# A Fourier filter and a gated feed-forward on one core: wider folding and filter operations, normalised rows kept in DRAM, eleven pairs of block products, and one written order

## The chip, the core and the metric

The kernel runs on one core of a Trainium2 chip. The time is device microseconds from the first to the last instruction of one execution; three runs of the kernel before gave 399.61, 400.31 and 401.77, and their median, 400.31, is what the change is measured against. One execution was also taken by the hardware profiler; its rows name the engines PE (matrix products), PEld (weight loads of PE), DVE (vector), ACT (scalar and activation), POOL (the third element-wise engine) and SP (which issues most DMA transfers).

## What is computed

```python
def _A_ref(x, w_r, w_i):                       # x: 1 x 2048 x 512
    X = rfft2(x) * (w_r + 1j * w_i)            # w: 2048 x 257
    return irfft2(X, (2048, 512))
def _B_ref(x, W_gate, W_up, W_down):           # F = 1376
    gate, up = x @ W_gate, x @ W_up
    return ((gate * (gate > 0)) * up) @ W_down

x = A_x
xn = _layernorm(x)
s = _A_ref(xn, A_w_r, A_w_i)
g = _silu(_B_ref(xn, B_W_gate, B_W_up, B_W_down))
return x + s * g
```

## The kernel before, in words

**Rows and blocks.** x is 2048 rows by 512 columns, held as 16 tiles of 128 rows. Two tiles together are a unit c = 0 … 7 of 512 KB: it is loaded, its mean and deviation are taken (`deviations`, L534), and `normalise` (L556) writes the normalised rows xf. Four tiles are a block of the feed-forward, c = 0 … 3.

**Numbers.** Every product has float16 operands. A float32 value is split into a high part (rounded to float16) and a low part (the rest), mostly a copy on ACT and a subtraction on DVE, and each product is done in three passes (`PASSES`: high·high, high·low, low·high).

**Feed-forward.** `turn` (L571) and `turn_row` (L632) make the transposed rows xT of a block. `product` (L953) multiplies them with gate and up weights (wgu), for 11 tiles f of 128 hidden columns (the last, TAIL, has 96): PE rows gu, groups of twelve matmuls 128x512. `hidden` (L1011) forms relu(gate)·up and splits it into h; `down` (L1032) multiplies h with the down weights wds into dn. The f tiles are taken in `PAIRS` (0,1), (3,4), (5,6), (7,8), (2,9). For some pairs and blocks `fast_products` (L1060) does not form the four products of twelve 512-wide matmuls but seven of twelve 256-wide ones (sa, sb, sc), by a scheme of Strassen's kind with sums and differences of row blocks (xS, made by `row_sums`, L595: sums on DVE, splits, two DMA writes to S_d and two transposing reads) and of weight blocks (wT and rp, made by `weight_sums`, L799). `FASTS` says for how many of the last blocks this is done, pair by pair.

**Filter branch.** The transform of the 512 columns and 2048 rows is done as products with small cosine and sine matrices. `fold` (L662) forms even and odd parts of xf (eo, ee, xs), `split` makes them float16, `first_stage` (L699) is the group s1 on PE (64-row products), whose results go to A_d in DRAM. Eight chunks q (`fft_chunk`, L1142) then load at from A_d and do y, xx, the filter (xsp, tt, pf), z and v, and store to C_d; the filter of a chunk is wt, scaled by cw (`filter_scale`, L895). `last_stage` (L1304) loads ct from C_d, does s2 on PE and unfolds it (zz, ae, ye, sv) to the rows s; `finish` (L1353) multiplies with the gate g and adds x. All eight first stages come before the first chunk, and all chunks before the first last stage; the feed-forward's products fill PE in between, so most filter steps lie on DVE, ACT and POOL while PE works on gu and dn.

**Order.** The functions do not issue instructions; they append steps (`step`, L236) with an engine, a cost, what they read and write, and a due time. `Plan.run` (L255) then places the steps: a list scheduler with modelled costs, a table DUES with a due time for each step, a table WAITS with the lead of loads, and rules for ports, buffers and changes of PE between 64-row and 128-row products. The result is the order in which instructions are issued to each engine, and each engine works through its own list in that order. Because all instructions go through one helper, most profile rows name its line, L200 before and L155 after.

Two short places say what the fast pairs are:

```python
def fast(c, n):
    return c >= NBL - int(FASTS[n])     # NBL = 4 blocks
FASTS = ['2', '1', '2', '2', '2']       # before: nine pairs
```

Of the kernel before, what the change touches and what calls it, by code (L numbers as in the profile page):

```python
# [1572 lines left out]
```

## Time and profile before

| what | value |
|---|---|
| runs | 399.61, 400.31, 401.77 us (median 400.31) |
| span of the profiled execution | 399.6 us |
| mean granted clock of PE | 0.996 |
| PE busy | 391.2 us (98%) |
| DVE busy | 329.2 us (82%), 726 instructions |
| ACT busy | 247.2 us (62%), 479 instructions |
| POOL busy | 72.3 us (18%), 79 instructions |
| DMA | 69.55 MB, 174 GB/s in the mean |

How to read the rows below. A row of the groups names line, engine, operation, output <- inputs, shape and count, and after the bar the busy time in us, the mean of one instruction in ns, and the idle time ahead of such instructions with what ended it. A row of a timeline has the start, the length in us, the engine, and how many instructions it joins. A row of the windows has the stretch in us, its length, the busy time of PE, PEld, DVE, ACT and POOL with instruction counts, the granted clock of PE, the DMA share and GB/s. Matmuls overlap, so the mean of one is longer than the distance between two.

### The profile page before, as it was taken

The page shows a single profiled execution, that of the slowest core. Times are in us where ns is not written, and L with a number is a line of the kernel's source. Part 1 is how long each engine was busy: PE and PEld are TensorE (multiplying, and loading weights), DVE is VectorE, ACT ScalarE, POOL GpSimd, SP SyncE. Part 2 cuts the span into 40 slices and gives each one's busy share as a digit, 9 for nine tenths or more (in the row PEclk, how much of TensorE's full clock was granted, in tenths as well). Part 3 has the DMA queues.
Part 4 walks back from the last instruction along what each step waited for, and adds up shares of the span by engine and source line. Part 5 has one row for each costly group of instructions (what it writes and reads, how often), then busy time and mean ns, then how long its engine had stood idle before and what let it go on. Part 6 is the DMA issues. An engine that isn't in the chain of part 4 may idle for free.

```text
span 399.6 us, 8608 instructions
## 1 busy us (share of the span) xinstructions
PE 391.2 (98%) x3332; PEld 243.8 (61%) x3332; DVE 329.2 (82%) x726; ACT 247.2 (62%) x479; POOL 72.3 (18%) x79
## 2 busy tenths in 40 slices
PE   6999999999999999999999999999999999999995
PEld 5965444544445444456585777776567878787544
DVE  3899998998888997669986888988769863887995
ACT  6997986868576666845568865535335542754422
POOL 1004300000000000051405391413212301122211
PEclk9899999999999999999999999999999999999999
DMA  7972311327812998997878790536543048998496
GB/s 272 407 230 63 106 54 34 100 55 178 294 55 51 307 307 244 279 268 167 215 222 246 223 241 22 146 81 199 153 125 107 2 106 183 228 296 167 133 239 158
DMA packets 59353, 69.55 MB, mean 174 GB/s; under 512 B 24688, under 2 KB 36560, under 8 KB 59312
## 3 DMA queue, kind: packets, MB, share of 16 engines
q1 hardware_dynamic: 57872, 66.38, 57.2%
q0 software_dynamic: 1440, 2.62, 4.3%
q8 instruction: 26, 0.43, 0.4%
q14 instruction: 15, 0.12, 0.1%
HBM read 43.81 MB, written 22.56 MB: 166 GB/s over the span
## 4 chain that ended last, share of the span: by engine, by line
PE 82%; DVE 8%; DMA 4%; ACT 3%; issue 2%; SPq 0%; DVEq 0%; ACTq 0%; POOLq 0%
PE dn L200 26%; PE gu L200 26%; PE sb L200 8%; PE sc L200 5%; PE sa L200 5%; PE z L200 3%; PE xx L200 3%; PE s L200 2%; DVE wgu L200 2%; PE y L200 2%; PE v L200 2%; DMA out<-sv 2%; DMA x<-in_x 2%; DVE sv L200 1%; ACT wgu L200 1%
## 5 line engine op out<-in xcount | busy, mean ns | idle before, releaser
L200 PEld LDWEIGHTS <-wgu 128*128 128x128 f16 x960 | 93.0, 98 | 65.3 <-issue 2.9
L200 PE MATMUL dn<-wds,h 128*128 128x512 f16 (+2 forms) x528 | 118.2, 373 | 0.3 <-DVE h L200 0.3
L200 PE MATMUL gu<-xT,wgu 128*128 128x512 f16 (+1 forms) x528 | 112.0, 369 | 0.4 <-DVE xT L200 0.4
L200 PEld LDWEIGHTS <-h 128*128 128x128 f16 (+1 forms) x594 | 53.5, 98 | 54.4 <-issue 2.8
L200 POOL TENSOR_TENSOR rp<-rp,rp 128x512 f32<-128x512 f32 x9 | 12.1, 1354 | 132.9 <-DVE pw L200 125.5
L200 PEld LDWEIGHTS <-wT 128*128 128x128 f16 x324 | 31.2, 98 | 6.1 <-issue 1.0
L200 PE MATMUL sb<-xS,wT 128*128 128x256 f16 x216 | 26.6, 273 | 0.0
L200 PE MATMUL sa<-xT,wgu 128*128 128x256 f16 x216 | 26.5, 273 | 0.0
L200 ACT ACTIVATE r<-gu 128x512 f32<-128x512 f32 (+2 forms) x26 | 14.9, 574 | 16.2 <-PE gu L200 16.2
L200 DVE TENSOR_TENSOR h<-gu,r 128x512 f32<-128x512 f32 (+3 forms) x34 | 20.6, 607 | 5.0 <-ACT h L200 3.5
L200 ACT ACTIVATE h<-h 128x512 f16<-128x512 f32 (+1 forms) x26 | 16.1, 624 | 11.8 <-DVE h L200 11.8
L200 DVE SCALAR_TENSOR_TENSOR tt<-xsp,cw,wt 128x512 f32<-128x512 f32 x32 | 22.8, 755 | 0.1
L200 ACT ACTIVATE g<-dn,cdi 128x512 f32<-128x512 f32 (+1 forms) x16 | 10.8, 673 | 16.5 <-PE dn L200 16.5
L200 DVE TENSOR_TENSOR h<-h,h 128x512 f16<-128x512 f32 (+1 forms) x26 | 18.3, 705 | 1.8 <-ACT h L200 1.7
L200 POOL TENSOR_TENSOR tt<-tt,tt 128x256 f32<-128x256 f32 x10 | 9.5, 957 | 43.1 <-DVE tt L200 41.1
L200 PE MATMUL gu<-xT,wgt 128*64 128x256 f16 (+1 forms) x144 | 17.0, 309 | 0.0
L200 ACT ACTIVATE a<-y 128x1024 f16<-128x1024 f32 x8 | 8.2, 1024 | 12.8 <-PE y L200 6.1
L200 DVE SCALAR_TENSOR_TENSOR wgu<-raw,p,wgu 128x512 f16<-128x512 f32 x20 | 15.1, 772 | 0.0
L200 POOL TENSOR_TENSOR pf<-tt,tt 128x256 f32<-128x256 f32 x12 | 11.3, 947 | 18.9 <-DVE tt L200 16.6
L200 DVE TENSOR_TENSOR a<-y,a 128x1024 f16<-128x1024 f32 x8 | 9.8, 1224 | 5.6 <-ACT a L200 5.5
L200 ACT ACTIVATE rp<-rp,csc 128x512 f32<-128x512 f32 x20 | 13.5, 713 | 1.1 <-DMA rp<-in_wg 1.1
L200 PEld LDWEIGHTS <-wgt 128*64 128x64 f16 (+1 forms) x144 | 9.6, 106 | 6.6 <-issue 1.3
(208 smaller groups left out, 701.2 us busy)
## 6 DMA issues: line engine op xcount, KB each, us to landing
A_d<-t SPq DMA_DIRECT2D x16, 256.0 KB, 3.8
rw<-in_wl SPq DMA_DIRECT2D x8, 512.0 KB, 5.2
wt<-in_wl SPq DMA_DIRECT2D x8, 512.0 KB, 5.5
at<-A_d SPq DMA_DIRECT2D x8, 512.0 KB, 5.1
C_d<-t SPq DMA_DIRECT2D x16, 256.0 KB, 3.5
ct<-C_d SPq DMA_DIRECT2D x16, 256.0 KB, 6.8
x<-in_x SPq DMA_DIRECT2D x7, 512.0 KB, 5.7
G_d<-g SPq DMA_DIRECT2D x12, 256.0 KB, 3.6
```

The source lines that it names most:

```text
L200: return lambda *args, **kw: self.tc.keep_in_program_order(f(*args, **kw))
```

## The change

**Eleven fast pairs.** `FASTS` becomes 2, 2, 2, 2, 3: pair (3,4) in block 2 and pair (2,9) in block 1 are now formed with seven block products too. For this, block 1 needs its row sums xS1, and the weight sums of pair (2,9) have to be there a block earlier.

**Wider folding.** Ten narrow additions and subtractions of `fold` (126 to 258 elements each) become six of 516, 516, 516, 516, 260 and 256, through views that run over both halves at once, some backwards. xs has 514 columns, and the constants are ordered to match.

**Rows away.** For c = 2 … 7 the normalised rows are written to N_d in DRAM and read back into a tile xg before they are folded, 512 KB each way.

**Wider filter.** Four scalar_tensor_tensor instructions of 512, four sums of 256 and four of 128 in each chunk become three scaled copies of the filter on ACT (512), two products of 1024, two sums of 512 and two of 256.

**Wider last stage.** Eight sums of 126 to 256 and two of 510 become two of 256, two of 512, one of 512 and one of 508.

**Order.** `Plan.run` no longer plans: it calls the steps in the order of a written list, ORDER, of step numbers, and for each step that several engines can do, a letter of PLACE (D, A, P) says which does it. More steps than before can go to POOL.

```diff
-FASTS = ['2', '1', '2', '2', '2']
+FASTS = '2,2,2,2,3'.split(',')
+AWAY = range(2, 8)
-DUES = (
-WAITS = (
...
+ORDER = (
+    4, 5, 6, 7, 8, 9, 10, 11, 12, 13, 14, 15, 16, 17, 18, 19, 46, 61, 47, 49, 71, 70, 1, 513, 62, 48, 53, 54, 89, 20, 21, 22, 23, 24, 25, 26, 27, 28,
...
+)
-RANGES = ((0, 257, 0), (257, 512, 1))
+RANGES = ((0, 257, 0, 0), (257, 512, 258, 1))
...
+    def either(self, options, reads=(), writes=(), **more):
+        place = next(self.places, None)
+        n = next((k for k, o in enumerate(options) if o[0][0] == place), 0)
+        engine, cost, fn, port = options[n]
+        s = self.step(engine, cost, fn, reads=reads, writes=writes, port=port, **more)
...
     def run(self):
-        steps = self.steps
...
-            order.append((t, s))
...
+        for n in ORDER:
+            self.steps[n].fn()
...
+    def both(n, fn, reads, writes, first="DVE", **more):
+        o = [("DVE", dve(n), lambda: fn(DVE), True), ("POOL", pool(n), lambda: fn(POOL), True)]
+        T.either(o if first == "DVE" else o[::-1], reads=reads, writes=writes, **more)
...
     def fold(c):
...
+        of = f"{'xg' if c in AWAY else 'xf'}{c}"
+        if c in AWAY:
+            tile_of(of, "k4", [P, 2, D + 2], F32)
+            step("SP", .6, lambda: SP.dma_start(N_d[c], T[f"xf{c}"][:, :, 0:D]), reads=[(f"xf{c}", 0), (f"xf{c}", 1)], writes=[("N_d", c)], kb=512)
+            step("SP", .6, lambda: SP.dma_start(T[of][:, :, 0:D], N_d[c]), reads=[("N_d", c)], writes=[(of, 0), (of, 1)], kb=512)
...
-        put("tensor_add", ev, (0, 257), xf, s(0, 257), xf, s(512, 255, -1), X + [(f"xf{c}", 2)], E)
-        put("tensor_sub", od, (1, 256), xf, s(1, 256), xf, s(511, 256, -1), X, O)
...
+        ends = lambda k: view(xf()[:, 0, 0:1], (D + 2, 2), ((256, -256)[k], 2), ((1, -1)[k], 129), at=D * k)
+        both(516, lambda e: e.tensor_add(eo()[:, :, 0], ends(0), ends(1)), X, [E[0]])
+        both(516, lambda e: e.tensor_sub(eo()[:, :, 1], ends(0), ends(1)), X, [E[1]])
...
     def fft_chunk(q, due):
...
-        for i, (ri, wi) in enumerate(((0, 0), (1, 1), (1, 0), (0, 1))):
-            step("DVE", stt(512), lambda i=i, ri=ri, wi=wi: DVE.scalar_tensor_tensor(
-                tt(i), xs().rearrange("p k g r c -> p (k g) r c")[:, :, ri, :], cw[:, wi:wi + 1],
...
+        for k, (to, i, by) in enumerate(((lambda: w2()[:, 0], 1, 2), (lambda: w2()[:, 1], 1, 1), (lambda: wt()[:, 0], 0, 0))):
+            step("ACT", act(512) + .1, lambda to=to, i=i, by=by: ACT.activation(to(), wt()[:, i], AF.Copy, scale=cw[:, by:by + 1]),
...
+        both(1024, lambda e: e.tensor_mul(flat(w2()), swap(), flat(w2())), [(xsn, 0), (xsn, 1), (w2n, 0), (w2n, 1)], [(w2n, 2)])
+        both(1024, lambda e: e.tensor_mul(own(), own(), flat(wt())[:, 0:1].broadcast_to([P, 2, D])), [(xsn, 0), (xsn, 1), (wtn, "w"), (w2n, 2), *keep], [(xsn, 2)])
+        both(512, lambda e: e.tensor_add(w5(1), own5(1), w5(1)), [(xsn, 2), (w2n, 2)], [(w2n, 3)])
+        both(512, lambda e: e.tensor_add(pf()[:, 0:8].rearrange("p k r c -> p r k c"), own5(0), w5(0)), [(xsn, 2), (w2n, 2)], [(pfn, 0)])
...
     def last_stage(c, due):
...
-        put("DVE", "tensor_add", lambda: yc()[:, :, 0:128], lambda: ac()[:, :, 0:128], b_, 256, C, (yen, 0))
...
+        both(512, lambda e: e.tensor_add(y()[:, :, :, 0, 0:128], *mid()), A, [(yen, 3)])
+        both(512, lambda e: e.tensor_sub(y()[:, :, :, 1, 0:128], *mid()), A, [(yen, 4)])
```

**The loads at the start.** SP's list before: after the first unit of x (two tiles) and the weights of the first tile f, three more units of x follow (x_157 and x_161 are units 2 and 3, x_177 is unit 1; rw is the filter, cS small constants).

```order
L200 DMA x_141<-in_x 128x512 x2
L200 DMA raw_0_148<-in_wg 128x512
L200 DMA raw_1_153<-in_wu 128x512
L200 DMA x_157<-in_x 128x1024
L200 DMA x_161<-in_x 128x1024
L200 DMA x_177<-in_x 128x1024
```

The same place after:

```order
L155 DMA x_164<-in_x 128x512 x2
L155 DMA raw_1_172<-in_wu 128x512
L155 DMA raw_0_174<-in_wg 128x512
L155 DMA cS<-in_c_s 128x7
L155 DMA rw_177<-in_wl 128x1024
L155 DMA x_166<-in_x 128x1024
```

Unit 1 (x_166) is now behind one filter load instead of behind units 2 and 3.

**ACT at the start.** ACT's list before, from the squares of the first weights on (xf_228 is the statistics of unit 2; xTf is the copy of the first transposed row tile, head, out of PSUM):

```order
L200 ACTIVATE wgu_94,m_201<-raw_1_153 128x512
L200 ACTIVATE q_191<-q_191 128x1
L200 ACTIVATE xf_228,st_229<-x_157 128x512
L200 ACTIVATE xTf_243<-head_231 128x512
L200 ACTIVATE xf_168<-x_141,q_191 128x512
```

And after:

```order
L155 ACTIVATE wgu_102,m_210<-raw_0_174 128x512
L155 ACTIVATE q_183<-q_183 128x1
L155 ACTIVATE xT_249<-xTf_236 128x512
L155 ACTIVATE xf_169<-x_164,q_183 128x512
L155 ACTIVATE junk_269,mw<-rw_177 128x1024
L155 ACTIVATE xTf_279<-head_226 128x512
```

The statistics of unit 2 are no longer ahead of the first row tile, whose copy (xTf_236) is now on DVE; the squares of a filter load (junk) come earlier.

**POOL in the chunks.** POOL's list before, in the first chunks after the weight sums: sums of 256 for the filter.

```order
L200 TENSOR_TENSOR pf_2387<-tt_1_2373,tt_1_2364 128x8x32
L200 TENSOR_TENSOR pf_2387<-tt_1_2366,tt_1_2341 128x8x32
L200 TENSOR_TENSOR tt_0_2465<-tt_0_2465,tt_0_2405 128x256
L200 TENSOR_TENSOR pf_2477<-tt_0_2465,tt_0_2405 128x8x32
L200 TENSOR_TENSOR tt_0_2496<-tt_0_2496,tt_0_2458 128x256
```

And after (xsp is the spectrum times the filter, w_0 the part with real and imaginary exchanged):

```order
L155 TENSOR_TENSOR xsp_2398<-xsp_2398,wt_2116 128x1024
L155 TENSOR_TENSOR w_0_2564<-xsp_2459,w_0_2564 128x2x256
L155 TENSOR_TENSOR pf_2632<-xsp_2459,w_0_2564 128x2x8x32
L155 TENSOR_TENSOR pf_2632<-w_0_2564 128x2x4x32
L155 TENSOR_TENSOR wT_110<-rp_1_2452,wT_110 128x512
```

POOL now has a product of 1024 elements, sums of 512, and low parts of weight sums (wT) in this stretch.

More of the change, by code (lines that the diff above doesn't have):

```diff
@@ L378, in pe, with view @@
     return n * (m / 2370 + .001)
+def view(a, *dims, at=0):
+    return bass.AP(tensor=a.tensor, offset=a.offset + at, ap=[list(a.ap[0]), *(list(d) for d in dims)])
 @with_exitstack
@@ L579, in turn @@
                  reads=[(f"xf{c}", i)], writes=[(f"x16_{c}", i, 0)])
-            e, cost = ((DVE, dve(512)), (POOL, pool(512)))[lows[i] == "POOL"]
-            step(lows[i], cost, lambda i=i, e=e: e.tensor_sub(x16()[:, i, 1, :], xf(i), x16()[:, i, 0, :]),
-                 reads=[(f"xf{c}", i), (f"x16_{c}", i, 0)], writes=[(f"x16_{c}", i, 1)], port=True)
+            both(512, lambda e, i=i: e.tensor_sub(x16()[:, i, 1, :], xf(i), x16()[:, i, 0, :]),
+                 reads=[(f"xf{c}", i), (f"x16_{c}", i, 0)], writes=[(f"x16_{c}", i, 1)])
         def run():
@@ L672, in fold @@
-        e, eng, cost = (("POOL", POOL, pool), ("DVE", DVE, dve))[FOLDS[c] == "DVE"]
-        step(e, (.35, .1)[e == "DVE"], lambda: eng.tensor_copy(xf()[:, :, D:D + 1], xf()[:, :, 0:1]), reads=X, writes=[(f"xf{c}", 2)], lead=FOLD0 if c < 2 else FOLD_LEAD)
-        def put(op, to, r, a, r1, b, r2, reads, write):
-            n = 2 * (r[1] - r[0])
-            step(e, cost(n), lambda: getattr(eng, op)(to()[:, :, r[0]:r[1]], a()[:, :, r1], b()[:, :, r2]),
-                 reads=reads, writes=[write], port=True, lead=FOLD0 if c < 2 else FOLD_LEAD)
@@ L816, in weight_sums @@
         G, U = ([(f"{raw}_{i}", j) for j in range(2)] for i in range(2))
-        eng, e, cost = (DVE, "DVE", dve(512)) if TSUMS[n] == "DVE" else (POOL, "POOL", pool(512))
         def minus(to, a, b, reads, name):
-            step(e, cost, lambda: eng.tensor_sub(B(*to), B(*a), B(*b)), reads=reads, writes=[name], port=True, due=due)
+            both(512, lambda e: e.tensor_sub(B(*to), B(*a), B(*b)), reads, [name], due=due)
         t1, t2, t3, t4 = ((t16, f"t{k}") for k in range(1, 5))
@@ L941, in corners @@
             DVE.tensor_sub(spw[:, 1], h4[:, 0], h4[:, 1])
-        step("DVE", .8, corners, reads=["s4", "cS"], writes=["spw"], due=due + 6)
+        step("DVE", .95, corners, reads=["s4", "cS"], writes=["spw"], due=due + 6, port=True)
     sums = {}
@@ L1104, in fast_products @@
         step("DVE", dve(512), lambda: DVE.tensor_mul(T[r1], T[B], T[r1]), reads=[B], writes=[r1], due=clock[0] + 3)
-        e, eng, cost = (("DVE", DVE, dve), ("POOL", POOL, pool))[SECONDS[5 * c + n] == "POOL"]
-        step(e, cost(512), lambda: eng.tensor_mul(T[E], T[E], T[r2]), reads=[r2], writes=[E], due=clock[0] + 3, port=True)
+        both(512, lambda e: e.tensor_mul(T[E], T[E], T[r2]), [r2], [E], due=clock[0] + 3)
         for m, h32 in enumerate((r1, E)):
@@ L1349, in last_stage, with copy @@
-        Y = [(yen, i) for i in range(6)]
-        put("DVE", "tensor_add", lambda: s()[:, :, 1:256], lambda: yc()[:, :, 1:256], lambda: ys()[:, :, 1:256], 510, Y, (sn, 0))
-        put("DVE", "tensor_sub", lambda: s()[:, :, 511:256:-1], lambda: yc()[:, :, 1:256], lambda: ys()[:, :, 1:256], 510, Y, (sn, 1))
+        z, ae, y, s = (lambda n=n: T[n] for n in (zn, aen, yen, sn))
+        at = lambda off, *dims: view(z()[:, 0, 0:1], (D, 2), *dims, at=off)
+        def copy(to, of, reads, write, **scale):
+            step("ACT", .11, lambda: ACT.activation(to(), of(), AF.Copy, **scale), reads=reads, writes=[write])
```

341 lines of the change are left out of this document (116 added, 225 removed), and 160 rows, old and new, of tables (DUES, ORDER, WAITS).

## The prediction

> **What bounds the kernel now.** I read the page first: the busy shares and the chain of waits.
>
> ```profile
> PE 391.2 (98%) x3332; PEld 243.8 (61%) x3332; DVE 329.2 (82%) x726; ACT 247.2 (62%) x479; POOL 72.3 (18%) x79
> ...
> PE 82%; DVE 8%; DMA 4%; ACT 3%; issue 2%; SPq 0%; DVEq 0%; ACTq 0%; POOLq 0%
> ```
>
> PE is busy for 391.2 of 399.6 us. So the time falls only by what PE has less to do, by what it stands at the start, and by what follows its last product. Work taken off DVE, ACT or POOL is worth nothing by itself; put late, it can only cost. The price of PE's work comes next, from groups by shape, and then from PE's timeline.
>
> ```profile
> L200 PE MATMUL gu<-xT,wgu 128*128 128x512 f16 x480 | 106.4, 379 | 0.1
> ...
> L200 PE MATMUL sb<-xS,wT 128*128 128x256 f16 x216 | 26.6, 273 | 0.0
> ```
>
> ```profile
> 202.54 1.47 PE L200 MATMUL sb<-xS,wT 128*128 128x256 f16 x12
> 203.85 1.47 PE L200 MATMUL sa<-xT,wgu 128*128 128x256 f16 x12
> 205.16 0.81 PE L200 MATMUL dn<-wds,h 128*128 128x512 f16 x3
> ...
> 210.62 2.76 PE L200 MATMUL gu<-xT,wgu 128*128 128x512 f16 x12
> 213.22 1.47 PE L200 MATMUL sc<-xT,wT 128*128 128x256 f16 x12
> ```
>
> The means (379 and 273 ns) overlap each other and are no price. Start to start, twelve 256-wide matmuls take 203.85 − 202.54 = 1.31 us and again 205.16 − 203.85 = 1.31; twelve 512-wide ones take 213.22 − 210.62 = 2.60.
>
> **Two more pairs by block products.** Block 2 pair (3,4) and block 1 pair (2,9) go from four groups of twelve 512-wide matmuls (4 × 2.60 = 10.40) to seven groups of twelve 256-wide ones (7 × 1.31 = 9.17): −1.23 each, **−2.5** for both, all on PE. What they need in return (row sums of block 1, weight sums of pair (2,9), some 20 DVE, ACT and POOL instructions and four transfers of 512 KB) lies beside PE if it is early enough; the rivals take up the case that it isn't.
>
> **Fewer changes between 64-row and 128-row products.** The written order of PE has 27 runs of 64-row products (y, v, s and the narrow gate tail) where there were 32, and 7 places instead of 4 where two s groups follow each other.
>
> ```profile
> 95.13 0.85 PE L200 MATMUL s<-xs,cR 64*64 64x257 f16 x24
> 95.91 8.60 PE L200 MATMUL dn<-wds,h 96*128 96x512 f16 x39
> 104.35 15.70 PE L200 MATMUL gu<-xT,wgu 128*128 128x512 f16 x72
> 119.98 1.51 PE L200 MATMUL s<-xs,cR 64*64 64x257 f16 x48
> 121.43 3.84 PE L200 MATMUL gu<-xT,wgu 128*128 128x512 f16 x17
> ...
> 188.58 1.48 PE L200 MATMUL sa<-xT,wgu 128*128 128x256 f16 x12
> 189.99 0.87 PE L200 MATMUL y<-cm,at 64*128 64x64 f16 x48
> ```
>
> The sa group of 1.31 us should end at 189.89, and y starts at 189.99: 0.10 per entry. A single s group takes 95.91 − 95.13 = 0.78, two in a row 121.43 − 119.98 = 1.45, so a pair saves 0.11. 5 × 0.10 + 3 × 0.11 = **−0.8** (bounds 0, if the runs are broken elsewhere, and −1.3, with as much again for leaving each run).
>
> **The start.** Three rows of PE carry idle time or a late arrival, two of ACT say why, and the windows show the rest.
>
> ```profile
> 9.94 3.26 PE L200 MATMUL gu<-xTf,raw 128*128 128x128 f32 x16 [1.40 <-ACT xTf L200]
> ...
> 17.69 1.04 PE L200 MATMUL head<-unit,xf 128*128 128x128 f32 x8
> ...
> 21.22 1.36 PE L200 MATMUL gu<-xT,wgu 128*128 128x256 f16 x11 [0.38 <-DVE xT L200]
> ```
>
> ```profile
> 8.68 0.63 ACT L200 ACTIVATE xf<-x 128x512 f32<-128x512 f32 x1 [1.09 <-DMA x<-in_x]
> ...
> 9.31 0.58 ACT L200 ACTIVATE xTf<-head 128x512 f32<-128x512 f32 x1
> ```
>
> ```profile
> 10.00:13.00 3.00, 3.00 (x17) 3.00 (x18) 2.90 (x7) 3.00 (x7) 0.00 (x0) 0.59 1.04 408
> 13.00:16.00 3.00, 3.00 (x22) 2.87 (x22) 2.00 (x8) 2.21 (x8) 0.00 (x0) 0.84 1.04 421
> ...
> 30.00:60.00 30.00, 29.94 (x151) 14.50 (x150) 28.84 (x81) 25.67 (x61) 8.47 (x11) 1.00 0.26 74
> 60.00:90.00 30.00, 30.00 (x197) 14.28 (x196) 28.64 (x56) 21.86 (x39) 0.00 (x0) 1.00 0.23 64
> ```
>
> ACT waits 1.09 us for a load of x and then does 0.63 of statistics before the copy that PE waits for. Now DVE does that copy and is not queued there, so PE begins some 1 to 1.4 us sooner. Loads of x2 and x3 (1 MB) stood ahead of x1; now one filter load (0.5 MB) does, and 0.5 MB at 408 GB/s is 1.3 us that x1, and the transposes at 17.69, gain on top. The most that can come of it: idle 1.40 + 0.38, and the clock's loss 3 × 0.41 + 3 × 0.16 = 1.7, together 3.5. But ACT gets squares for later weight groups placed earlier, and with its instructions up to there put end to end, each at its duration in this trace (0.63 for such a pass, row 8.68), it then holds PE three times before 35 us (0.9, 0.6, 0.6); after that DVE's list is as full as before (28.84 and 28.64 of 30). I take **−1.5**, bounds 0 and −3.5.
>
> **The tail.**
>
> ```profile
> 392.73 2.24 PE L200 MATMUL dn<-wds,h 128*128 128x256 f16 x19
> ...
> 395.01 0.47 ACT L200 ACTIVATE g<-dn,cdi 128x256 f32<-128x256 f32 x1 [2.92 <-PE dn L200]
> 395.51 0.42 DVE L200 TENSOR_TENSOR sv<-sv,g 128x256 f32<-128x256 f32 x1 [1.05 <-ACT g L200]
> 395.97 0.42 DVE L200 TENSOR_TENSOR xt<-xt,sv 128x256 f32<-128x256 f32 x1
> ```
>
> Behind the last product come a gate, two DVE instructions and a store, at 256 columns. The written order ends with a piece of 128: 0.11 less on ACT and 0.12 less on each DVE instruction, **−0.4** (0 to −0.6 with a shorter store).
>
> **Filter, folding and last stage.** The narrow instructions pay a fixed part, and the wide ones pay it once.
>
> ```profile
> L200 DVE SCALAR_TENSOR_TENSOR tt<-xsp,cw,wt 128x512 f32<-128x512 f32 x32 | 22.8, 755 | 0.1
> ...
> L200 DVE TENSOR_TENSOR h<-gu,r 128x512 f32<-128x512 f32 x20 | 13.6, 686 | 4.9 <-ACT h L200 3.5 <-ACT r L200 0.7 <-PE gu L200 0.5
> ...
> L200 DVE TENSOR_TENSOR xs<-xs,xs 128x1024 f16<-128x1024 f32 x8 | 9.8, 1222 | 4.1 <-ACT xs L200 4.1
> ...
> L200 POOL TENSOR_TENSOR rp<-rp,rp 128x512 f32<-128x512 f32 x9 | 12.1, 1354 | 132.9 <-DVE pw L200 125.5 <-ACT rp L200 7.1
> ...
> L200 POOL TENSOR_TENSOR rp<-rp 128x512 f32<-128x512 f32 x3 | 5.0, 1664 | 0.2
> ```
>
> From 686 ns at 512 and 1222 at 1024, DVE's fixed part is 150 ns; 116 fewer DVE instructions (726 to 610) save 17 us. POOL gets about 33 us more, by its order at these durations; at 1.3 us per 512 there for 0.69 on DVE that is 17 more off DVE. The two pairs add some 6. So DVE loses about 28 and ACT gains some 18 (three scaled copies per chunk). On the end that is worth **0** by itself, since PE covers it; it buys lead. A 1024-wide two-input instruction on POOL, which four chunks now have in the chain from xx to z, isn't in the trace: two of 1.35 (2.7) to two of 1.66 (3.3), for 1.22 on DVE. I take 2.7, nearest to the nine common ones. For stalls where such a result comes late I add **+0.6**, bounds 0 and +8.4 (below).
>
> Does POOL slow DVE? Two rows of DVE and one of POOL:
>
> ```profile
> 224.46 0.42 DVE L200 TENSOR_TENSOR wgu<-rp,wgu 128x256 f16<-128x256 f32 x1
> ...
> 233.04 1.48 DVE L200 TENSOR_TENSOR wgu<-rp,wgu 128x256 f16<-128x256 f32 x1
> ```
>
> ```profile
> 232.11 2.13 POOL L200 TENSOR_TENSOR rp<-rp 128x512 f32<-128x512 f32 x1
> ```
>
> The same instruction takes 0.42 alone and 1.48 when it begins within POOL's, ending 0.3 behind it: 1.06 lost. The Trainium skill (SBUF — State Buffer, Who interferes with whom) states that a DVE instruction with two SBUF inputs and a GpSimd instruction that reads SBUF take turns, whole instruction by whole instruction, and this row agrees. By that rule taken to its end, each added POOL instruction would cost DVE its whole length, 33 us together, and the sum stays as it is while DVE is under PE.
>
> By the rows alone: 1.06 on each of some 25 instructions (33 / 1.35) is 26 us, all of POOL's added time 33; DVE then has 329 − 28 + 26 = 327, or 334 at worst, under PE's 388 (391.2 − 2.5 − 0.8). It does not become the bound as a whole, only in stretches.
>
> **Rows away to DRAM.** Six tiles of 512 KB go out and come back, 6 MB.
>
> ```profile
> x<-in_x SPq DMA_DIRECT2D x7, 512.0 KB, 5.7
> ...
> 150.00:180.00 30.00, 30.00 (x293) 15.14 (x292) 20.92 (x42) 19.91 (x34) 5.56 (x4) 1.00 0.95 263
> ```
>
> One such transfer takes 5.7 us, the round trip at least 11.4. SP issues in order, so a reload that waits for its store holds up the loads of weights and of x behind it, and PE's next block waits for those. Between 30 and 90 the DMA share is 0.26 and 0.23; there it is free. At 150 to 180 (0.95) it isn't, but by then only the last tiles travel. I take **0**; if one reload in that stretch is late by a whole transfer, +5.7.
>
> **The sum.** 399.6 − 2.5 − 0.8 − 1.5 − 0.4 + 0.6 = 395.0 of span. The span profiled equals the fastest run shown (399.61), and the median, 400.31, is 0.7 above; so 395.0 + 0.7 = **395.7**.
>
> **Rivals.** (1) The start gives all: PE never waits on ACT in the first 35 us and later steps keep the lead. −3.5 for −1.5, no stalls: 392.4 + 0.7 = 393.1. For it: DVE's list shrinks; against: ACT was already at 25.67 of 30. (2) The block products save little: taken from the busy time per matmul (26.6/216 = 0.123, 106.4/480 = 0.222), seven groups cost 84 × 0.123 = 10.3 against 48 × 0.222 = 10.6, −0.3 each; with the start lost to ACT, 399.6 − 0.6 − 0.4 = 398.6, and 399.3. Against it stand the start-to-start times. (3) Slower: the filter chain on POOL. In four chunks a 1024-wide step at up to 3.3 for 1.22 makes z 2.1 us late, with the port loss of 1.06 up to 3.2; PE takes its products in the written order and stands for whatever exceeds the lead. At 2.1 each 395.0 − 0.6 + 8.4 = 402.8, and 403.5; at 3.2 it is 407.9. It decides from about 1.1 us a chunk (no longer 0.5% faster), and is slower than before by 0.5% from 2 us. For it: POOL's instructions are twice as long; against: before, the same products waited behind four 755 ns instructions and POOL sums without PE idle. (4) The reloads collide: +5.7, 400.7, and 401.4, no difference.
>
> **Chances.** My forecast (394 to 398) 0.52, (1) 0.20, (2) 0.09, (3) 0.12, (4) 0.07. A difference under 0.5% (2 us) can't be told from none. Faster by over that: forecast and (1), 0.72; within: (2) and (4), 0.16; slower: (3), 0.12. The range reaches from below (1) to between (2) and (4): 391.5 to 400.5.
>
> **What would show it.** The plain group of gu by wgu has 384 matmuls for 480 and sb by xS and wT 264 for 216, with twelve of them still 1.31 start to start. PE's first f32 product begins before 9 us, the transposes of 17.69 before 16.5; by 35 us PE is 1.5 ahead. DVE near 300 us busy and below 26 of 30 from 60 on; POOL near 105. The chain stays PE at over 80%. I am wrong if PE shows idle time of over 1 us behind pf, p or xs between 100 and 330 (rival 3), or behind a load (rival 4), or if the start lies later than before.

## The result and the profile after

The changed kernel takes 398.25 us (median of nine runs, 397.61 to 398.86); nine runs of the kernel before beside them have a median of 400.21 (399.56 to 401.77). The ratio is 0.9944 (0.9928 to 0.9959): faster by 0.56%, about 2 us. The forecast was 4.6 us. The profiled execution took 398.29, with a span of 396.5.

The page after, its busy times and its chain of waits:

```profile
PE 387.1 (98%) x3404; PEld 251.0 (63%) x3404; DVE 313.6 (79%) x610; ACT 260.8 (66%) x512; POOL 103.7 (26%) x92
...
PE 66%; DMA 8%; DVE 3%; ACT 3%; SPq 1%; issue 1%; POOL 0%; DVEq 0%
```

PE has 4.1 us less to do than in the first profile of before and is still the bound. The chain's 66% can't be set against the 82% of before as it stands: followed back from the end, this chain breaks off at 66.8 us, and over the 330 us that it covers PE has 79%. What PE waits for, by tile; the columns are total, count and longest wait in us. First after, then a second profiled execution of the kernel before (`before_again`):

```profile
PE sb L155 <- ACT sb L155: 1.5, 1, 1.5
PE small L155 <- DVE md L155: 1.1, 1, 1.1
PE gu L155 <- ACT r L155: 1.0, 1, 1.0
PE dn L155 <- DVE wds L155: 0.9, 1, 0.9
PE s L155 <- DMA ct<-C_d: 0.4, 1, 0.4
```

```profile
PE small L200 <- DVE md L200: 1.1, 1, 1.1
PE small L200 <- ACT wgu L200: 0.8, 1, 0.8
PE gu L200 <- ACT xTf L200: 0.7, 1, 0.7
PE gu L200 <- DMA raw<-in_wu: 0.6, 1, 0.6
PE gu L200 <- DVE xT L200: 0.4, 1, 0.4
```

The wait behind md is in both, at the very beginning. In before_again all the others lie in the first 22 us, and after that PE doesn't stop (in the first execution it does once, 0.3 at 378). After, the start has none of them, and four new ones lie later. PE's timeline after, at the start and at the first three of those (rows with f32 are products on float32 operands, so not every product is float16):

```profile
8.83 2.05 PE L155 MATMUL gu<-xTf,raw 128*128 128x128 f32 x16
...
13.94 1.04 PE L155 MATMUL head<-unit,xf 128*128 128x128 f32 x8
...
79.06 0.59 PE L155 MATMUL dn<-wds,h 128*128 128x512 f16 x2 [0.85 <-DVE wds L155]
...
103.97 1.24 PE L155 MATMUL gu<-xT,wgu 128*128 128x512 f16 x5 [1.02 <-ACT r L155]
...
217.92 1.47 PE L155 MATMUL sb<-xS,wT 128*128 128x256 f16 x12 [1.49 <-ACT sb L155]
219.22 1.04 PE L155 MATMUL sa<-xT,wgu 128*128 128x256 f16 x8
```

The fourth, 0.4 behind a load of ct, comes at 345. Call the three others A (78), B (103) and C (217).

**Where the time went.** I added up PE's timeline from the start of one matmul to the start of the next, so that each microsecond belongs to one kind of work or to a stall. In us:

| | before | before_again | after |
|---|---|---|---|
| start to the first 512-wide gu | 25.40 | 24.76 | 20.40 |
| later gu, sa, sb, sc | 197.76 | 197.76 | 196.64 |
| 64-row products | 31.25 | 31.25 | 30.93 |
| entries into them (31, 31, 22) | 2.90 | 2.94 | 2.06 |
| dn, xx, z and the rest | 136.94 | 137.07 | 137.49 |
| stalls after the start | 0.46 | 0.00 | 4.21 |
| from the last matmul's start on | 4.85 | 4.71 | 4.80 |
| span | 399.55 | 398.48 | 396.53 |

The first two rows belong together, since twelve 256-wide gu products (1.3 us) have moved from the first into the second: by their number (96 fewer of 512 at 0.216, 168 more of 256 at 0.109) the products lose 2.4, and the rest of the two rows' difference, 3.1 against before_again, is the start. So: products −2.4, start −3.1, 64-row products and their entries −1.2, stalls +4.2, rest +0.5, together −2.0. **Of the 6.7 us that PE gained, 4.2 are lost again in stalls.** The comparison goes against before_again, because its time (400.3 for a span of 398.5) is next to the median. The first profiled execution was 1.1 slower, 0.6 of it at the start and 0.5 in the stall at 378. PE's clock was 0.59 and 0.84 in two stretches of its start (the rows are in the prediction), and 1.00 here:

```profile
10.00:13.00 3.00, 2.49 (x20) 2.25 (x20) 2.75 (x8) 3.00 (x8) 0.00 (x0) 1.00 1.02 393
13.00:16.00 3.00, 2.80 (x23) 2.71 (x24) 2.86 (x11) 2.81 (x10) 0.00 (x0) 1.00 1.04 423
```

**What is late at A, B and C.** DVE and POOL after, ahead of A:

```profile
73.64 0.43 DVE L155 TENSOR_TENSOR xs<-ee 128x260 f32<-128x260 f32 x1
...
75.27 1.75 DVE L155 TENSOR_SCALAR scd<-rho,pd 128x11 f32<-128x11 f32 x1
...
78.26 0.74 DVE L155 SCALAR_TENSOR_TENSOR wds<-wds,scd 128x512 f16<-128x512 f32 x1
```

```profile
74.92 2.07 POOL L155 TENSOR_TENSOR xs<-xs,xs 128x1028 f16<-128x1028 f32 x1 [2.61 <-ACT xs L155]
```

The tensor_scalar of eleven elements takes 1.75 us: it begins within POOL's subtraction for the fold and ends with it. The scaled down weights wds, which PE waits for, come four instructions later. ACT after, ahead of B and of C:

```profile
101.77 1.06 ACT L155 ACTIVATE xs<-xs 128x1028 f16<-128x1028 f32 x1 [1.37 <-DVE xs L155]
102.73 0.71 ACT L155 ACTIVATE wds<-wds,scd 128x512 f16<-128x512 f32 x1
103.35 0.57 ACT L155 ACTIVATE r<-gu 128x512 f32<-128x512 f32 x1
...
215.05 0.59 ACT L155 ACTIVATE r<-gu 96x512 f32<-96x512 f32 x1 [2.90 <-PE gu L155]
215.54 0.62 ACT L155 ACTIVATE h<-sr 128x512 f16<-128x512 f32 x1
216.06 1.32 ACT L155 ACTIVATE rp<-rp,csc 128x512 f32<-128x512 f32 x2
217.29 0.58 ACT L155 ACTIVATE sb<-sa 128x512 f32<-128x512 f32 x1
```

At B, ACT stands 1.37 us for DVE's folded xs; r, which empties the gate sums out of PSUM and lets PE go on, is two instructions behind. At C, ACT stands 2.90 for the narrow gate tail, and the copy of sa, which PE needs to go on, is four instructions behind. My theory: C is a matter of ACT's written order alone; A and B come from DVE being full between 60 and 125, and a later result has no lead there. The rivals: A and B are also just order; or PE simply arrives there earlier than DVE can be (the start's 3 us are given back); or rows away or the wide POOL steps cause them.

The windows of DVE in that stretch, after and before_again (the third busy time is DVE's, the last POOL's):

```profile
60.00:90.00 30.00, 29.05 (x176) 13.48 (x174) 28.62 (x68) 22.76 (x49) 9.83 (x8) 1.00 0.68 193
90.00:120.00 30.00, 28.98 (x193) 13.83 (x191) 27.07 (x68) 25.21 (x49) 4.16 (x4) 1.00 0.79 237
```

```profile
60.00:90.00 30.00, 30.00 (x196) 14.20 (x195) 28.31 (x57) 21.39 (x38) 0.00 (x0) 1.00 0.25 66
90.00:120.00 30.00, 30.00 (x177) 13.80 (x179) 25.49 (x76) 21.23 (x44) 0.00 (x0) 1.00 0.58 172
```

From 60 to 90 DVE was as full before, without a stall of PE; POOL did nothing there then. Being full is therefore not enough. What differs too is the lead of the scale scd, on which wds and so every dn product depends. In before_again:

```profile
62.34 0.23 DVE L200 TENSOR_SCALAR scd<-rho,pd 128x11 f32<-128x11 f32 x1
...
66.71 2.11 PE L200 MATMUL dn<-wds,h 128*128 128x512 f16 x9
```

There scd is done 4.1 us before the first dn product; after, it is done at 77.02, 0.8 before the first dn at 77.83, since the written order prepares the down weights later. My reading is that a full DVE takes away the room in which a late result can be made up for; an earlier place for the whole preparation of the down weights, which would test the other reading, was not tried.

### The profile page after: what moved, and what is told of

The parts are those of the page before. It is cut to its first block, busy times and chain, and to the rows that moved or that the text cites. A ratio compares the mean times of both kernels' runs of the same rounds, so it can differ in the third digit from the quotient of the medians.

```text
span 396.5 us, 8764 instructions
## 1 busy us (share of the span) xinstructions
PE 387.1 (98%) x3404; PEld 251.0 (63%) x3404; DVE 313.6 (79%) x610; ACT 260.8 (66%) x512; POOL 103.7 (26%) x92
## 4 chain that ended last, share of the span: by engine, by line
PE 66%; DMA 8%; DVE 3%; ACT 3%; SPq 1%; issue 1%; POOL 0%; DVEq 0%
PE dn L155 26%; PE sb L155 9%; PE gu L155 7%; PE sa L155 6%; PE sc L155 6%; DMA ct<-C_d 5%; PE z L155 3%; PE xx L155 3%; PE y L155 2%; DMA xS<-S_d 2%; PE v L155 2%; PE s L155 2%; DMA A_d<-t 1%; SPq L155 1%; DVE xs L155 1%
## 5 line engine op out<-in xcount | busy, mean ns | idle before, releaser
L155 PE MATMUL gu<-xT,wgu 128*128 128x512 f16 (+1 forms) x432 | 90.8, 367 | 1.0 <-ACT r L155 1.0
L155 PEld LDWEIGHTS <-wT 128*128 128x128 f16 x396 | 38.5, 98 | 7.8 <-issue 2.3
L155 PE MATMUL sa<-xT,wgu 128*128 128x256 f16 x264 | 32.5, 273 | 0.0
L155 DVE TENSOR_TENSOR t<-v,t 128x1024 f16<-128x1024 f32 x8 | 9.7, 1222 | 10.2 <-ACT t L155 10.2
L155 PE MATMUL sb<-xS,wgu 128*128 128x256 f16 x132 | 16.2, 273 | 0.0
L155 PE MATMUL sc<-xS,wgu 128*128 128x256 f16 x132 | 16.2, 273 | 0.0
L155 PE MATMUL sc<-xT,wT 128*128 128x256 f16 x132 | 16.2, 273 | 0.0
L155 ACT ACTIVATE sq<-sc 128x512 f32<-128x512 f32 x11 | 6.5, 591 | 13.7 <-PE sc L155 8.9
L155 POOL TENSOR_TENSOR h<-h,h 128x512 f16<-128x512 f32 (+1 forms) x6 | 7.8, 1301 | 23.9 <-ACT h L155 23.9
L155 DVE TENSOR_TENSOR w<-xsp,w 128x1024 f32<-128x1024 f32 (+1 forms) x12 | 12.0, 999 | 2.5 <-POOL xsp L155 2.2
```

Of the source, the lines that this page charges most:

```text
L155: return lambda *args, **kw: self.tc.keep_in_program_order(f(*args, **kw))
```

## The experiments

Each is a change to the changed kernel, except the first. The ratios are against the kernel before on the same chip; the changed kernel itself has 0.9944 (0.9928 to 0.9959), 398.25 us. Differences in us are between medians. The kernel before had medians from 399.89 to 400.31 beside the experiments, so by the ratios a difference comes out up to 0.7 us higher (4.8 for 4.1 in `dve_chunks`), and one under about 1 us is not told apart from none.

**The kernel before, once more**, to see how its executions differ. No edit.

> The kernel before, unchanged. The changed kernel's runs lie 1.7 to 1.8 us above their spans (398.29 with a span of 396.5), and I had taken 0.7 for the kernel before (400.31 against 399.6). Theory: the execution of before that was profiled was one of its slow ones, and what lies around a span is the same 1.75 for both: its runs then have spans of about 398.5 with times of about 400.2. Rival: the kernel before has less around its span: spans of about 399.5 with times of 400.2.

399.88 us, 0.9992 of itself. Its profiled span is 398.5, 1.1 below the first one, at a mean clock of 0.999 for 0.996. In the runs of the same kernel beside it the two with 0.996 have spans of 399.7 and 399.9, and those from 0.997 up lie between 397.5 and 398.8. Among the ten of the experiment itself one with 0.996 has 398.1, so the clock does not explain all of it. The execution on which I based the sum was one of the few long ones, and the 1.8 us around the span are the same for both kernels, so the time is not only the stretch from the first to the last instruction.

**A: the fold's subtraction from POOL to DVE**, behind the first wds.

```diff
 DVE:
 L155 SCALAR_TENSOR_TENSOR wds<-wds,scd 128x512
+L155 TENSOR_TENSOR xs_1_1021<-xs_953,xs_1_1021 128x2x514
 POOL:
-L155 TENSOR_TENSOR xs_1_1021<-xs_953,xs_1_1021 128x2x514
```

> The changed kernel with one step moved: the low part of xs for unit 1 (1028 elements wide) is done by DVE behind the first low part of the down weights, not by POOL ahead of it. In the changed kernel DVE's scd takes 1.75 us beside POOL's instruction (74.92 to 76.99), the low part of wds comes late and PE stands 0.85 at 79.06. Theory (the port, and stalls add up on PE): scd takes 0.3, PE's wait for wds at about 78 falls under 0.3, and the time falls by 0.7 to 1.0, to about 397.4. Rival (PE is only ahead of DVE here, which is the bound): PE's wait moves to a later product and the time stays at 398.2 within 0.3.

399.15 us, 0.9978 (0.9959 to 0.9998), 0.9 slower than the change. A is gone, and PE waits three times just behind it, 0.59, 0.23 and 0.46. The first of these, and what ACT and DVE do ahead of it:

```profile
83.78 1.04 PE L155 MATMUL dn<-wds,h 128*128 128x512 f16 x3 [0.59 <-DVE h L155]
...
79.19 1.06 ACT L155 ACTIVATE xs<-xs 128x1028 f16<-128x1028 f32 x1 [2.01 <-issue]
...
80.28 1.23 DVE L155 TENSOR_TENSOR xs<-xs,xs 128x1028 f16<-128x1028 f32 x1 [1.17 <-ACT xs L155]
```

The block had cost DVE about 1.5 (1.75 for an instruction of 0.23), and the subtraction costs it 1.22, so with both it is level with the changed kernel: it ends the moved subtraction at 79.11, where the changed kernel ends that wds at 79.00. What it loses comes next. Ahead of the fold's high part for another unit ACT stands 2.01 us, until just behind the end of the moved subtraction (the profile names no releaser), and DVE, which needs that high part, stands 1.17. What is queued behind is over 1 us late, ACT's h among it (80.77 for 79.67). So the repair lost to a new wait between ACT and DVE, and not to a lack of room on DVE.

**A: POOL earlier**, by DVE making the statistics (st) for which ACT stands four instructions earlier.

```diff
 DVE:
 L155 TENSOR_SCALAR wide_md<-unit,md 128x128
+L155 TENSOR_SCALAR st_969<-st_969 128x2
 L155 TENSOR_TENSOR ee_964<-eo_918 128x4x129
...
-L155 TENSOR_SCALAR st_972<-st_972 128x2
```

> The changed kernel with no work moved between engines: on DVE the small statistics step of unit 4 (st, for which ACT stands 3.06 us at 72.38 with the high part of xs queued behind) comes ahead of four folding and splitting steps, not behind them. POOL's low part of xs (2.07 us) then starts about 2.5 us earlier, and no longer beside DVE's scd, which took 1.75 there. Theory (the stall at 79 comes from the place of that one POOL instruction): PE's wait on wds there falls under 0.4, and the time falls by 0.5 to 1.0, to 397.3 to 397.8. Rival (DVE has no room in this stretch, whoever waits): the wait only moves, and the time stays within 0.4 of 398.25.

398.26 us, 0.995 (0.9932 to 0.9968): no difference. POOL began 1.6 earlier, at 73.30, and what it met on DVE was another instruction:

```profile
73.98 2.12 DVE L155 TENSOR_TENSOR xs<-ee 128x260 f32<-128x260 f32 x1
...
77.31 0.23 DVE L155 TENSOR_SCALAR scd<-rho,pd 128x11 f32<-128x11 f32 x1
```

scd now takes its 0.23, and the sum of 260 takes 2.12 where it took 0.43. The wait at 78 stays at 1.0, with 0.3 more just ahead of it. The block cost DVE 1.7 in the one place and 1.5 in the other.

**A: what PE needs earlier on DVE and ACT**, scd and the first wds ahead of the fold; on ACT the first high part of wds also moves ahead of two statistics passes.

```diff
 DVE:
-L155 TENSOR_TENSOR xs_999<-eo_835 128x2x2x129
-L155 TENSOR_TENSOR xs_999<-ee_981 128x4x65
...
 L155 TENSOR_SCALAR scd<-rho,pd 128x11
+L155 TENSOR_TENSOR xs_1053<-eo_835 128x2x2x129
...
+L155 SCALAR_TENSOR_TENSOR wds<-wds,scd 128x512
 L155 TENSOR_TENSOR h_0_5_854<-h_0_5_812,h_0_5_854 128x512
-L155 SCALAR_TENSOR_TENSOR wds<-wds,scd 128x512
+L155 TENSOR_TENSOR xs_1053<-ee_981 128x4x65
```

> The changed kernel with DVE's scale of the down weights (scd, which needs the maximum over rows that PE delivers at 69.9) and the first low part of wds ahead of the last folding sums of unit 0, and ACT's first high part of wds ahead of two statistics passes. What was seen so far: at the other place POOL's instruction just blocked another DVE instruction (2.12 for 0.43), and PE stood 1.01 as before. Theory (PE waits for one late result behind 4 us of DVE queue; POOL's block only decides which step is late): PE's wait on wds near 78 goes and the time falls by 0.6 to 1.0, to about 397.5. Rival (this stretch of DVE is full, so what is done earlier makes its neighbours late): waits of 0.8 or more appear on s, h or wds before 90, and the time stays within 0.4 of 398.25.

399.32 us, 0.9982 (0.9967 to 0.9996). The wait at 78 is gone, and three stand behind it again (0.62, 0.23, 0.46 from 83.9 on); POOL's subtraction met the very wds that was moved:

```profile
75.80 2.05 DVE L155 SCALAR_TENSOR_TENSOR wds<-wds,scd 128x512 f16<-128x512 f32 x1 [0.20 <-ACT wds L155]
```

Here too ACT stands 1.81 for a folding sum that has moved behind on DVE (it ends at 79.20, ACT starts at 79.28), and DVE then stands 1.17 for ACT. Three repairs of one wait, and none wins; but in two of them DVE had 1.17 us of idle time behind the move, so they don't show that it had no room. They show that each place tried for these steps makes a neighbour late.

**B: r ahead of the fold's copy on ACT.**

```diff
 ACT:
+L155 ACTIVATE r_3_1393<-gu_3_0_1245 128x512
 L155 ACTIVATE xs_3_1395<-xs_1373 128x2x514
 L155 ACTIVATE wds<-wds,scd 128x512
-L155 ACTIVATE r_3_1404<-gu_3_0_1245 128x512
```

> The changed kernel with one step moved: ACT rectifies gate tile 3 of block 1 (r, whose product was done long before) ahead of the high part of xs for unit 3, not behind it. There ACT stands 1.37 us for DVE's xs with r queued behind, and PE stands 1.02 at 103.97 for the PSUM buffer that r frees. Theory: PE's wait on ACT r goes, the time falls by 1.0 to 1.2, to about 397.1. Rival (DVE is the bound in this stretch, 27 of 30 us): the wait returns within 20 us behind another operation, and the time stays at 398.2 within 0.3.

398.44 us, 0.9951 (0.9929 to 0.9972): no difference. The wait at 103 is gone; PE waits 0.23 at 114 behind DVE's wds and then here, where ACT has a table load of 1.28 us ahead of g:

```profile
123.91 1.45 PE L155 MATMUL dn<-wds,h 128*128 128x512 f16 x6 [0.59 <-ACT g L155]
```

This execution also waited 1.5 at the start, which has nothing to do with the edit, so its span can't say what the edit was worth. From the start of one matmul to the next, the two waits are 0.40 and 0.75, together as long as B was (1.19): it has moved, not gone. The gain of 1.0 to 1.2 that the theory had did not come; a gain of some tenths the runs can't exclude.

**C: the copy of sa earlier on ACT.**

```diff
 ACT:
 L155 ACTIVATE wt_2566<-wt_2566,cw 128x512
+L155 ACTIVATE sb_1_2853<-sa_1_2814 128x512
 L155 ACTIVATE rp_1_2576<-rp_1_2576,csc 128x4x128
...
-L155 ACTIVATE sb_1_2906<-sa_1_2814 128x512
```

> The changed kernel with one step moved: ACT's copy of sa to sb in pair (3,4) of block 2, one of the two new pairs, is done before two scalings and the rectifying of the gate tail, not behind them. There ACT stands 2.90 us for the tail's product with the copy queued behind, and PE stands 1.49 at 217.92 for the copy. Theory: the wait goes, and the time falls by 1.5 to 1.7, to about 396.6. Rival (the filter chain of chunks 2 and 3 is late anyway and PE would meet it next): a wait of over 1 us appears before 250 and the time falls by under 0.5.

397.68 us, 0.9928 (0.9907 to 0.995). C is gone (sb starts at 216.72, 1.32 behind sc), and PE waits 0.56 at 220 for the chunk's t, whose copy out of PSUM is still behind on ACT, and 0.27 at 224. In place of C's 1.66 (from start to start) stands 0.72 at 220; the time, 0.6 lower, is not told apart from none.

**C: and t earlier too.**

```diff
 ACT:
+L155 ACTIVATE sb_1_2853<-sa_1_2814 128x512
...
 L155 ACTIVATE h_2_0_0_2899<-sr_0_2794 128x512
+L155 ACTIVATE t_0_2901<-v_2856 128x2x512
 L155 ACTIVATE rp_0_2725<-rp_0_2725,csc 128x4x128
 L155 ACTIVATE rp_1_2538<-rp_1_2538,csc 128x4x128
-L155 ACTIVATE sb_1_2906<-sa_1_2814 128x512
-L155 ACTIVATE t_0_2908<-v_2854 128x2x512
```

> The changed kernel with two ACT steps moved: the copy of sa to sb as in the run with that alone (which fell 0.6 only, with a new wait of 0.72 on t behind it), and the high part of t of chunk 0, now ahead of two scalings. Theory: both waits go, and the time falls by 1.3 to 1.7, to about 396.7. Rival: another wait takes their place before 250 and the time stays near that of the single move, 397.7.

**396.78 us, 0.9914 (0.9895 to 0.9932)**, the best of all and ahead of both kernels. PE's waits are now

```profile
PE small L155 <- DVE md L155: 1.1, 1, 1.1
PE gu L155 <- ACT r L155: 1.0, 1, 1.0
PE dn L155 <- DVE wds L155: 0.8, 1, 0.8
PE y L155 <- ACT rp L155: 0.5, 1, 0.5
```

C was order: ACT works in order, and an instruction that nobody urgently needed stood for PE's tail ahead of two that PE needed. The stalls fall from 4.21 to 2.67, and the median by 1.5 (1.2 by the ratios). Of the stalls C's 1.66 are gone and the wait for ct too, which comes and goes from execution to execution, and 0.5 behind ACT's rp is new.

**The third repair of A and both of C together.** The two edits shown.

> The changed kernel with the moves of the last run and the two ACT moves in pair (3,4) of block 2 (396.8 alone, 1.5 less). If stalls add up on PE: 395.8 to 396.2. If the first stretch is full: 396.8 as before.

398.15 us, 0.9951 (0.9935 to 0.9967): 1.4 slower than the repair of C alone, as the edit at A was 1.1 slower by itself.

**Does PE just arrive too early?** Twenty idle products more on PE, 2.2 us, ahead of its first data product. In the profiled execution that product starts only 1.08 later (9.92 for 8.83), because the idle products ahead of them were done 0.9 sooner than in the changed kernel's execution.

```diff
 ORDER:
-    ..., 42, 43, 44, ...
+    ..., 42, 43, 43, 43, ... (20 more), 44, ...
```

> The changed kernel with 20 more idle products of 128x256 on PE (0.109 us each, 2.2 us in all) ahead of its first product of data; nothing else is delayed by it directly. Theory 1 (after the better start, DVE and ACT set the pace between 40 and 125 us, and PE's three waits there only give the start's gain back): PE's waits at 78 and 103 shrink by about 2 us together and the time rises by under 0.8, from 398.25 to at most 399.0. Theory 2 (PE sets the pace, and each stall is a late result of its own): the waits stay and the time rises by 2.0 to 2.2, to about 400.4.

399.35 us, 0.9982 (0.997 to 0.9993), 1.1 slower than the change, between the two forecasts; A and B stay (0.8 and 0.8 in the view of waits). PE comes to A 1.1 later and waits as long: the start's gain is real time, and A and B are not its return.

**The load of x1 late**, behind 1.28 MB of weights, to see the same with a real cause.

```diff
 SP:
-L155 DMA x_166<-in_x 128x1024
 L155 DMA raw_0_185<-in_wg 128x512
 L155 DMA raw_0_197<-in_wg 128x1024
 L155 DMA raw_1_211<-in_wu 128x1024
+L155 DMA x_166<-in_x 128x1024
```

> The changed kernel with the load of unit 1 of x behind three loads of weights (1.28 MB) instead of ahead of them: at 415 GB/s, 3.1 us later. Theory (the order of the first loads gives the start's gain, and it is kept to the end): the transposes of unit 1 (13.94) and all after them are 2.5 to 3.1 later, and the time rises by 2.2 to 3.1, to about 401. Rival (the start's gain is given back by 125 us): PE's waits between 70 and 125 vanish and the time rises by under 1.2.

402.64 us, 1.0056 (1.0038 to 1.0073): 4.4 more than the change, all of it at the start, with B (1.0) and A (0.8) as they were.

```profile
17.30 1.94 PE L155 MATMUL head<-unit,xf 128*128 128x128 f32 x8 [3.02 <-DVE xf L155]
```

```profile
16.00:30.00 14.00, 12.70 (x83) 9.95 (x84) 11.79 (x33) 12.21 (x33) 1.15 (x1) 0.88 0.83 288
```

The wait is 3.02, and the lower clock after it costs 14 × 0.12 = 1.7 more.

**Less for DVE in the stretch**: pair (2,9) in block 1 plain again.

```diff
-FASTS = '2,2,2,2,3'.split(',')
+FASTS = '2,2,2,2,2'.split(',')
```

> The changed kernel with pair (2,9) of block 1 done by plain products again (ten pairs), at the places of its block products; the row sums of block 1 fall away (on DVE, ACT and POOL some 9 us, 2 MB of transfers), the pair's weight sums stay, since blocks 2 and 3 use them. By PE's start-to-start times alone the time rises by 1.2, to 399.5 (theory 2). By theory 1 PE gets 1.2 more to do in a stretch where it waits, and DVE and ACT get less: the time stays or falls by up to 1.5, to 396.8 to 398.4.

399.07 us, 0.9976 (0.9965 to 0.9987), 0.8 slower than the change (1.3 by the ratios). By the products alone it should be 1.2 slower. DVE's window and PE's are here

```profile
60.00:90.00 30.00, 30.00 (x183) 14.26 (x182) 26.93 (x68) 21.64 (x48) 8.18 (x7) 1.00 0.34 115
```

PE is busy throughout: A is gone with 1.7 us less on DVE, although POOL's subtraction blocks scd for 1.75 here as well; scd just comes 2.4 us earlier (72.89). B stays (0.7), and new waits stand between 158 and 164 (1.2 behind ACT's g), so that the sum of the stalls is the same, 4.4 for 4.2. The pair pays what its products save, and removing it takes A away but not the stalls.

**More for DVE**, 8.4 us each time by the forecast: twelve of the fold's sums eo done twice (between 56 and 145), or seven of the chunks' sums pf three times (between 185 and 309).

```diff
 ORDER (first kernel):
-    ..., 190, ...
+    ..., 190, 190, ...
 ORDER (second kernel):
-    ..., 1261, ...
+    ..., 1261, 1261, 1261, ...
```

> The changed kernel with 12 of the folding's additions and subtractions of 516 elements on DVE done twice (the same result), from units 0 to 7, between 55 and 125 us: 12 x 0.70 = 8.4 us more on DVE there. Theory 1 (DVE sets the pace in this stretch): the time rises by 3 to 8 us, to 401 to 406, with PE waiting on DVE. Theory 2 (DVE is covered by PE, its time worth nothing): by under 1 us, to at most 399.2.

> The changed kernel with the filter's sum of 512 elements done three times instead of once in the seven chunks in which DVE does it: 14 x 0.6 = 8.4 us more on DVE between 165 and 320 us, 1.2 in the chain of each chunk. Both theories: here DVE is busy 18 to 25 of 30 us and the result is early, so the time stays within 0.5 of 398.25. If instead the filter's chain is what PE waits for next in the chunks, each of the seven adds up to 1.2, and the time rises by 2 to 8.

403.76 us (1.0093; 1.0066 to 1.012) and 402.39 (1.0064; 1.0044 to 1.0084): 5.5 and 4.1 more than the change. The first waits of each in the view of PE's waits:

```profile
PE gu L156 <- DVE h L156: 2.2, 2, 2.0
PE rows_md L156 <- DVE wide_md L156: 2.1, 1, 2.1
PE dn L156 <- DVE wds L156: 2.0, 2, 1.1
```

```profile
PE sb L156 <- DVE sc L156: 3.0, 2, 1.9
PE sb L156 <- ACT sb L156: 1.7, 2, 1.5
PE z L156 <- DVE t L156: 1.1, 1, 1.1
```

DVE's busy time rises by 9.7 and 11.3 (from 313.6 to 323.3 and 324.9), so a microsecond of it, in these places, goes with 0.57 and 0.36 us of the end. With DVE busy for 79% of the span, PE covers only part of it. The second kernel also makes the chain of each of seven chunks some 1.4 longer, and the run doesn't separate that from DVE's time; of the two cases in its expectation (within 0.5, or each chunk adding its part) the second came.

**The wide filter steps back to DVE**: the four 1024-wide ones that POOL does (xsp twice, w, p).

```diff
 POOL:
-L155 TENSOR_TENSOR xsp_2398<-xsp_2398,wt_2116 128x1024
...
 DVE:
 L155 TENSOR_SCALAR az<-a_0_2333,cS 128x2x2 x2
+L155 TENSOR_TENSOR xsp_2398<-xsp_2398,wt_2116 128x1024
```

> The changed kernel with the four 1024-wide instructions of the filter chains that POOL does (chunks 1, 4, 5, 6) done by DVE at the same places: 4 x 1.22 more on DVE, 4 x about 2.5 less on POOL. My rival 3 of the prediction (PE waits for the long POOL step): the time falls by 1 to 4, to 394 to 397. If DVE's time is what the chunks live on, as the run with 8.4 us more on DVE (4.1 longer) suggests, POOL is where these steps should be: the time rises by 1 to 2.4, to 399 to 400.6. No difference (within 0.4) if neither is near the path.

397.87 us, 0.9933 (0.9918 to 0.9948), with A, B and C as they were: no difference. DVE is busy 4.1 us more (317.7) and POOL 9.5 less, so in the chunks this much of DVE's time costs nothing that shows where the chain gets shorter by it. That the steps cost nothing on POOL either is not shown by the time alone, since two costs could cancel; but in the changed kernel PE has no wait behind them.

**No rows away**: the fold reads xf, and nothing goes to N_d.

```diff
-AWAY = range(2, 8)
+AWAY = range(0)
```

> The changed kernel with no rows sent away: folding reads the normalised rows from where they were made, the order of all other steps is as it was, 12 transfers of 512 KB (6.3 MB) fall away, and the rows hold their buffers (10 of this size for all) until folded. My prediction had 0 for the trip: the time within 0.5 of 398.25. If the trip makes the folding late (DVE stands 0.83 for a transfer out of such a buffer at 99.6): 1 to 2 faster. If the buffers are what it was for: later steps wait for a free one and the time rises by 2 or more.

397.77 us, 0.9935 (0.991 to 0.996), with the same waits, A and B among them. Six round trips of 512 KB cost and bring nothing beyond the 1 us that the runs can tell apart.

## Why the prediction was right and wrong

The time, 398.25, lies within the range and on the side forecast; the size, −2.0 for −4.6, does not fit. By the terms:

| term | forecast | measured |
|---|---|---|
| two pairs | −2.5 | −2.4 |
| 64-row products and their entries | −0.8 | −1.2 |
| start | −1.5 | −3.1 |
| tail | −0.4 | +0.1 |
| stalls | +0.6 | +4.2 |
| other work of PE | 0 | +0.4 |
| sum | −4.6 | −2.0 |

**The step that failed is the stalls**, +0.6 by the prediction and +4.2 in the trace, and with it the sentence that DVE's load is "worth 0 by itself, since PE covers it". The bounds (0 and +8.4) held 4.2, but I put it in the wrong place: in the chunks' filter chain on POOL. The filter steps on POOL cost nothing that shows (`wide_dve`). What cost was the wider folding on POOL, whose block hits DVE just ahead of the wds that PE needs (A, 1.0), the fold's copy on ACT ahead of r (B, 1.2), an ACT order in a new pair beside the chunks (C, 1.7), and a late load of ct (0.6). That C was order and worth its length is shown. Why A and B can't be moved away is in part argued: a full DVE, and the short lead that the written order leaves scd. For A's part I had the rows: I quoted DVE's 28.84 and 28.64 of 30 between 30 and 90 and read them as cover. A full engine is cover only for what is due late; and in `dve_front` a microsecond there goes with 0.57 us of the end. I also expected DVE below 26 of 30 from 60 on and near 300 us in all; it has 28.6 and 27.1 there, and 313.6. The chain of waits, forecast at over 80% on PE, has 79% over the part that it covers. By the prediction's own sign of being wrong, idle time of over 1 us behind xs between 100 and 330, B counts: 1.02 at 104, behind ACT's wait for xs. Rival (3)'s limit of 1.1 us a chunk was also summed wrongly: 395.1 + 4 × 0.8 = 398.3 is already 0.5% under the time before, so the limit is 0.8.

**The pairs** came out as worked out: 384 plain products and 264 of sb, still 1.30 from start to start (217.92 to 219.22). Rival (2), −0.3 each by busy times, falls. **The entries**: the trace has 31 before and 22 after, not 32 and 27, and 0.094 each, not 0.10; the count was wrong, the mechanism right. **The start** gave twice what I took, near rival (1), though not to be read too finely from one execution (the same row is 19.97 to 21.35 in the experiments that don't touch the start): the three holds by ACT before 35 us (0.9, 0.6, 0.6), found by putting durations end to end, did not come. PE's first f32 product began at 8.83, the transposes at 13.94, as forecast and better. Rival (1) needed "no stalls" as well, and those came. **The tail** won nothing that shows: behind the last piece the gate and both DVE instructions are shorter, but from the last matmul's start to the end it is 4.80 for 4.71 (3.9 to 5.2 in the profiles of the experiments):

```profile
391.99 0.37 ACT L155 ACTIVATE g<-dn_3b,cdi 128x128 f32<-128x128 f32 x1 [1.18 <-PE dn_3b L155]
...
392.39 0.29 DVE L155 TENSOR_TENSOR sv<-sv,g 128x128 f32<-128x128 f32 x1
392.72 0.29 DVE L155 TENSOR_TENSOR xt<-xt,sv 128x128 f32<-128x128 f32 x1
```

xt ends at 393.01 and the span at 396.5, 3.5 later; before it was 396.39 and 399.6, 3.2. Why the store of half the width takes no less was not tried.

**Rows away** at 0 was right, and rival (4) falls (`no_away`). **Rival (3)** falls in its place, the filter, though its mechanism, wide POOL steps that make something late for PE, is part of A. **POOL on DVE**: all POOL's added time on DVE, 33 us, was the extreme. Adding up what the DVE instructions that overlap POOL's two-input ones took above the shortest of their operation and shape in the trace, one gets 15.2 us in before_again and 16.0 after, and 17.5 with scd, which has no second of its kind; POOL's two-input instructions took 62.4 and 95.7 us. So 33 us more on POOL cost DVE some 2. **The base**: I took the profiled span of before as typical and added 0.7; it was 1.1 above the second one, and the runs lie 1.8 above their span. The two errors cancel, by luck. That the time fell on the side forecast is not luck, since products, entries and start came as forecast or better; that it stayed within the range owes something to the start, which gave 1.6 more and paid for part of the stalls.

What stays open: what A and B are worth together if scd had its old lead, or DVE more room. Each repair moved the wait, none ended it.

## What to carry to other kernels

A share of 80% for an engine that isn't the bound is no cover in itself; look at the windows, and where they are full, price what is due there and look how long before its use it is made. When PE stops behind an engine that works in order, look what that engine stood for: if it is a result nobody needs yet, moving two rows wins the stall (C, 1.5 us), while in a stretch where several engines wait on each other a moved row can just move the stall (A, three times, twice because ACT then stood some 2 us for a step that the edit had put back). And take the base of a sum from several executions, at the clock that most of them have.
